# Channel attention on one core: how much of the packed blocks' room joins the ring of the second pass, and in what order rows leave

## The chip, the cores and the metric

One core of a Trainium2 chip runs the kernel; the other cores are idle. The metric is the device time of one execution in microseconds (us). A row below means one row of every partition: 128 pixels of 384 channels in bf16, 98,304 bytes. The input has 1152 such rows (113.25 MB), the output as many.

## The reference

```python
xf = x.reshape(B, H * W, C)          # x: (1, 384, 384, 384) bf16
gap = jnp.mean(xf, 1)
gmp = jnp.amax(xf, 1)
h_a = gap @ w1;  h_a = h_a * (h_a > 0)
h_m = gmp @ w1;  h_m = h_m * (h_m > 0)
scale = sigmoid(h_a @ w2 + h_m @ w2)
return x * scale[:, None, None, :]
```

The scale of each channel needs the mean and the maximum over all pixels, so every pixel must be seen before the first one can be multiplied. x doesn't fit on the chip's SBUF whole.

## The kernel before

**First pass.** All 1152 rows are read (SP issues, L356). For each piece PE adds the rows up (`sums`, L259), and DVE keeps a running maximum in `acc` (L325). What fits stays on the chip: the three slots of `body` (96 rows, `STAYING`), 21 rows in `held`, 11 in `acc`, 8 + 2 in PSUM, a few more, and seven *packed blocks*. A packed block is 32 rows kept in the room of 24: four parts a, b, w, d of 8 rows (G = 8) each. PE and ACT turn the high bytes of the four parts into codes of 4 bits, four codes to a 16-bit word, and the fourth part gives up its own room (`pack`, L301; its room in `held` is used again by the next block). 782 rows are let go and have to be read again (`PLACES`, `again`).

**Turn.** After the last row the mean, the maximum and the two small products give `scale_bc` (L387 to L417).

**Second pass.** `multiply` (L422, DVE) scales rows in place; stores are issued by ACT (`put`, L431; `store`, L474), reads by SP (`read`, L506). First the staying rows leave (`put`), in small pieces at the start (`FIRST_STORES`). As their room comes free, the 782 rows are read again into places of `body` that are handed out in the order of `PLACES`: this is the ring. Its turn number k takes the next place in order, multiplies, stores, issues the reads that have become possible, and then does the turn's job of `jobs`:

- `unpack(i, h)` (L446): half a packed block back to four parts: eight DVE operations (L452, L457), six copies on ACT (L471). Part d goes to a home in `held`, two homes in turn (`homes_d`).
- `finish(i)` (L478): multiplies the block's 24 rows and the 8 rows of part d, and stores both. After it the block's 24 rows of `body` may join the ring: `read` compares a place's end with `RING + 3 * G * blocks_gone`.

So the ring begins with 96 rows (RING) and grows by 24 with each finished block, and the later entries of `PLACES` are longer: 24, 30, 36, 48 rows, the last one 20. At turn 19 (`LEAVING_TURN`) the rows that were kept in PSUM are copied or multiplied into rows 222 and up of `body` (L549 to L553), and they are stored with the next turns. Everything on an engine stays in the written order (`manual_schedule`). Every DMA reports to one of eight semaphores in turn, and the issue of a DMA also waits until the one that had its semaphore before has landed. Last stands a branch (L555) that is taken only if the values didn't fit the packing; with this input it is not taken.

Of the kernel before, what the change touches and what calls it, by code (L numbers as in the profile page):

```python
# [32 lines left out]
RING = 96  # L33
G = 8
PACKED = 7
PSUM_ROWS = 8
LATE_ROWS = 8
BANK_ROWS = 2
# [14 lines left out]


PLACES = (
# [3 lines left out]
)  # L59
LEAVING_AT = 222  # L60
LEAVING_TURN = 19
FIRST_STORES = ((1, 2, 3, 4, 4, 5, 6, 6), (9, 10, 12), (16, 18))
HELD_STORES = (6, 7)
ACC_STORES_AT = 3
# [6 lines left out]
def kernel(  # L71
# [7 lines left out]
    nc = tc.nc  # L79
# [11 lines left out]
    xr = x.rearrange("b h w c -> (b h w) c")  # L91
    orr = out.rearrange("b h w c -> (b h w) c")

    def rows_of(ap, block):
        first, n = block
        return ap[first * P:(first + n) * P, :].rearrange("(p n) c -> p n c", n=n)
# [8 lines left out]
    def take(n):  # L105
        nonlocal at
        at += n
        return at - n, n

    ps_block = take(PSUM_ROWS)  # L110
    beside = take(BANK_ROWS + A)
    packed_block = take(GP * PACKED)
    held_block = take(sum(LAST_HELD))
# [7 lines left out]
    again = [take(n) for _, n in PLACES]  # L121


    small = consts.tile([P, 16], BF16)
# [18 lines left out]
    acc = consts.tile([P, A, C], BF16)  # L143
    nc.dynamic_dma_scratch_size = RING_BYTES
    nc.lookup_mloc("DynamicDMAScratchLoc").dims = [P, RING_BYTES]
    held = nc.alloc_sbuf_tensor_at("held", [P, HELD_ROWS, C], BF16, offset=RING_BYTES).ap()
    body = xpool.tile([P, RING + 3 * G * PACKED, C], BF16, name="body")
    slots = [body[:, SLOT * i:SLOT * i + stay[i][1], :] for i in range(NS)]
    spare = body[:, SLOT * NS, :]
    homes = [body[:, RING + 3 * G * i:RING + 3 * G * (i + 1), :] for i in range(PACKED)]  # L150
# [10 lines left out]
    kept_ps = psum.tile([P, PSUM_ROWS, C], BF16)  # L161
    words_ps = psum.tile([P, G, C], BF16)
    words = words_ps.rearrange("p n c -> p (n c)").bitcast(F32)
    late = words_ps[:, 0:LATE_ROWS, :]
# [7 lines left out]
    kept_b = bank_b[:, 0:C * BANK_ROWS // 2].bitcast(BF16).rearrange("p (n c) -> p n c", n=BANK_ROWS)  # L172
# [5 lines left out]
    in_order.enter_context(tc.manual_schedule(engines=None))  # L178

    nc.vector.memset(ones_bf, 1.0)  # L180
    nc.vector.memset(pick, 0.0)
    for q in range(CQ):
        nc.vector.memset(pick[q * QP:q * QP + 1, q:q + 1], 1.0)
# [32 lines left out]
    for i in range(PACKED):  # L216
        first, d_at = 3 * G * i, 3 * G * PACKED + G * i
# [20 lines left out]
    for block, buf, pieces in parts_left:  # L238
        for j, m in enumerate(pieces):
            lo = sum(pieces[:j])  # L240
# [86 lines left out]
    def turn_over(out_, rows):  # L327

        for r in range(LATE_ROWS):
            for q in range(CQ):  # L330
                nc.tensor.transpose(  # L331
                    out=out_[:, r, q * P:(q + 1) * P], in_=rows[:, r, q * P:(q + 1) * P], identity=ident_bf
                )
# [11 lines left out]
    for st in steps:  # L345
# [8 lines left out]
        _, block, rows, lo, hi = st  # L354
        m = hi - lo
# [8 lines left out]
        j = max(0, min(m, A - done))  # L364
# [41 lines left out]
    for q0, part_ps in tp_ps:  # L406
        n = part_ps.shape[1]
# [12 lines left out]
    def multiply(dst, src):  # L420
        n = dst.shape[1]
        nc.vector.tensor_tensor(  # L422
            out=dst, in0=src, in1=scale_bc.unsqueeze(1).to_broadcast([P, n, C]), op=ALU.mult
        )
# [13 lines left out]


    turns = len(PLACES)  # L440
    homes_d = [held[:, G * ((i + 1) % 2):G * ((i + 1) % 2 + 1), :] for i in range(PACKED)]
    HG = G // 2
    m = held[:, 2 * G:2 * G + HG, :]
    t = acc[:, G:G + HG // 2, :].rearrange("p n c -> p (n c)").bitcast(U8)
# [28 lines left out]
    def store(buf, block, lo):  # L473
        nc.scalar.dma_start(out=rows_of(orr, block)[:, lo:lo + buf.shape[1], :], in_=buf)  # L474

    d_at = 3 * G * PACKED

    def finish(i):  # L478

        for rows in (homes[i], homes_d[i]):  # L480
            multiply(rows, rows)
        store(homes[i], packed_block, 3 * G * i)
        store(homes_d[i], packed_block, d_at + G * i)


    jobs = [[(unpack, 0, 0)], [(unpack, 0, 1)]]
    for i in range(1, PACKED):
        jobs += [[(unpack, i, 0)], [(finish, i - 1)], [(unpack, i, 1)]]
    jobs.append([])
    jobs.append([(finish, PACKED - 1)])  # L490

    order = []
    turn_of_row = [-1] * (RING + 3 * G * PACKED)

    def read(last_turn, blocks_gone):

        if not again:
            return False
        k = len(PLACES) - len(again)
        lo, n = PLACES[k]  # L500
        if lo + n > RING + 3 * G * blocks_gone or max(turn_of_row[lo:lo + n]) > last_turn:
            return False
        turn_of_row[lo:lo + n] = [k] * n
        buf, b = body[:, lo:lo + n, :], again.pop(0)
        assert b[1] == n
        nc.sync.dma_start(out=buf, in_=rows_of(xr, b))  # L506
        order.append((b, buf))
        return True

    k = ACC_STORES_AT  # L510
    put(stay[0], slots[0], FIRST_STORES[0][:k])
    put_acc()
    j = sum(FIRST_STORES[0][:k])
    put(stay[0], slots[0][:, j:, :], FIRST_STORES[0][k:], j)
    put(held_block, held[:, LATE_ROWS:, :], HELD_STORES, LATE_ROWS)
    put(refill, held[:, 0:LATE_ROWS, :], (LATE_ROWS,))
    read(-1, 0)
    put(stay[1], slots[1], FIRST_STORES[1])
    read(-1, 0)
    put(stay[2], slots[2], FIRST_STORES[2])  # L520
    read(-1, 0)
    read(-1, 0)
    nc.vector.tensor_scalar(out=flag, in0=bad_ps, scalar1=0.5, scalar2=None, op0=ALU.is_gt)
    bad = nc.values_load(flag, engines=(ENG.SP, ENG.Activation, ENG.DVE))
    assert len(jobs) <= turns - 2
    leaving = []
    gone = 0
    for turn in range(turns):
        b, buf = order.pop(0)
        multiply(buf, buf)  # L530
        store(buf, b, 0)
        if leaving:
            to, block = leaving.pop(0)
            store(to, block, 0)
        while read(turn, gone):
            pass
        for job, *which in jobs.pop(0) if jobs else ():
            job(*which)
            gone += job is finish
        if turn == LEAVING_TURN:  # L540
            j = LEAVING_AT
            assert j >= max(lo + n for lo, n in PLACES) and gone > PACKED - 2
            for block, rows in ((ps_block, kept_ps[:, 0:PSUM_ROWS, :]), (held_block, late), (beside, kept_b)):
                n = rows.shape[1]
                leaving.append((body[:, j:j + n, :], block))
                j += n
            assert j <= RING + 3 * G * (PACKED - 1)
            to = leaving[1][0]
            nc.vector.tensor_copy(out=to.bitcast(U32), in_=late.bitcast(U32))  # L549
            turn_over(late, to)  # L550
            multiply(leaving[0][0], kept_ps[:, 0:PSUM_ROWS, :])
            multiply(leaving[2][0], kept_b)
            multiply(to, late)  # L553
    assert not again and not order and not jobs and not leaving
    with tc.If(bad != 0):  # L555
        for i in range(PACKED):
            for buf, lo in ((homes[i], 3 * G * i), (homes_d[i], d_at + G * i)):
                n = buf.shape[1]
# [33 lines left out]
```

## Time and profile before

| | |
|---|---|
| time, median of 3 (lowest to highest) | 731.45 us (731.15 to 733.26) |
| time of the profiled execution | 731.59 us |
| its span, first to last instruction | 729.8 us |
| busy in the span: DVE, ACT, PE | 563.1, 348.7, 186.4 us |
| moved by DMA | 305.63 MB, mean 419 GB/s over the span |
| of it read, written | 192.14 MB, 113.25 MB |
| second pass: first read issued, last read landed, last store issued | 290.1, 687.2, 696.2 us |

The profile gives busy times by engine, and the DMA's by sixteen DMA engines that share every transfer: a DMA share of 1.00 in a stretch means that all sixteen had a packet in hand all the time (it can come out a little above 1, because a packet is counted in the stretch in which it starts). GB/s beside it is what they moved. A wait names what ended it.

### The profile page before, as it was taken

The numbers are of one execution on the slowest core, as the hardware profiler recorded it, in microseconds if no ns is written. First come the engines' busy times: TensorE is split into PE (matmuls) and PEld (weight loads), VectorE is DVE, ScalarE is ACT, GpSimd is POOL, SyncE is SP. The second block draws the span as 40 slices with busy tenths as digits, with TensorE's granted clock in tenths as the row PEclk, the third lists the DMA queues.
The fourth block names the chain that finished last, engine by engine and source line by source line (L and its number), as shares of the span: only waits on it lengthen the run. The fifth ranks groups of instructions, "written<-read, shape, count | busy, mean of one in ns | idle before, by whom it ended". The sixth has DMA issues, their size and how long they took to land.

```text
span 729.8 us, 3860 instructions
## 1 busy us (share of the span) xinstructions
PE 186.4 (26%) x1357; PEld 73.0 (10%) x1357; DVE 563.1 (77%) x421; ACT 348.7 (48%) x251; POOL 0.7 (0%) x6
## 2 busy tenths in 40 slices
PE   5667576876768470000000000000000000010000
PEld 2222222322222140000000000000000000010000
DVE  6799999999999998959999595975865790059910
ACT  6979999999999100047245345080080063000000
POOL 0000000000000000000000000000000000000000
PEclk9878977998897555555555555555555555555555
DMA  9999999999999979999999999999999999999996
GB/s 381 434 425 419 438 420 439 423 434 425 426 430 423 418 298 356 395 434 425 433 427 438 434 424 429 431 438 425 435 435 428 431 431 443 419 436 425 430 423 293
DMA packets 21987, 305.63 MB, mean 419 GB/s; under 512 B 2800, under 2 KB 3408, under 8 KB 9552
## 3 DMA queue, kind: packets, MB, share of 16 engines
q1 hardware_dynamic: 13328, 192.14, 62.2%
q10 hardware_dynamic: 8640, 113.25, 36.4%
q8 instruction: 10, 0.16, 0.1%
q14 instruction: 9, 0.07, 0.0%
HBM read 192.14 MB, written 113.25 MB: 418 GB/s over the span
## 4 chain that ended last, share of the span: by engine, by line
DMA 59%; DVE 23%; another core or an unknown queue 6%; issue 3%; PE 2%; ACT 1%; SPq 0%; ACTq 0%; DVEq 0%
DMA body<-in_x_dram 42%; DMA out_dram<-body 17%; DVE body L422 11%; DVE acc L325 10%; PE words_ps L307 1%; PE bank_a L259 1%; DVE held L422 1%; ACT body L471 0%; ACT held L471 0%; SPq L356 0%; PE words_ps L331 0%; DVE acc L422 0%; DVE held L452 0%; DVE body L549 0%
## 5 line engine op out<-in xcount | busy, mean ns | idle before, releaser
L422 DVE TENSOR_TENSOR body<-body,scale_bc 128x9216 bf16<-128x9216 bf16 (+15 forms) x45 | 214.5, 4802 | 63.0 <-DMA body<-in_x_dram 60.2
L325 DVE TENSOR_TENSOR acc<-acc,body 128x2304 bf16<-128x2304 bf16 (+4 forms) x210 | 229.7, 1166 | 14.6 <-DMA body<-in_x_dram 14.5
L471 ACT COPY held<-body 128x1536 uint8<-128x1536 uint8 x14 | 20.6, 1475 | 202.8 <-DMA out_dram<-held 131.5
L259 PE MATMUL bank_a<-body,small 128*1 128x512 bf16 (+2 forms) x849 | 93.0, 481 | 83.8 <-DMA body<-in_x_dram 83.7
L331 PE MATMUL words_ps<-ident_bf,body 128*128 128x128 bf16 x24 | 2.7, 309 | 370.9 <-DVE body L549 370.9
L287 ACT ACTIVATE held<-held 128x3072 uint8<-128x3072 uint8 (+1 forms) x35 | 82.0, 2344 | 1.1
L286 ACT ACTIVATE held<-body,held 128x3072 uint8<-128x3072 int8 (+1 forms) x28 | 61.9, 2211 | 10.5 <-DMA body<-in_x_dram 10.0
L259 PEld LDWEIGHTS <-small 128*1 128x1 bf16 x891 | 30.4, 96 | 147.1 <-issue 131.6
L471 ACT COPY body<-acc 128x1536 uint8<-128x1536 uint8 x28 | 41.2, 1472 | 0.4
L331 PEld LDWEIGHTS <-body 128*128 128x128 bf16 x24 | 2.5, 144 | 371.2 <-issue 371.2
L307 PE MATMUL words_ps<-body,scale_bc 128*128 128x512 fp8e4 (+1 forms) x126 | 37.4, 409 | 3.7 <-ACT body L314 3.7
L549 DVE COPY body<-words_ps 128x1536 uint32<-128x1536 uint32 x1 | 1.8, 1757 | 43.5 <-DMA out_dram<-body 43.5
L307 PE MATMUL words_ps<-body,w_sb 128*128 128x512 fp8e3 x84 | 26.0, 392 | 0.0
L307 PE MATMUL words_ps<-held,body 128*128 128x512 fp8e4 x84 | 25.0, 379 | 0.0
L471 ACT COPY held<-acc 128x1536 uint8<-128x1536 uint8 x14 | 20.6, 1472 | 6.1 <-DVE acc L457 6.1
L471 ACT COPY body<-body 128x1536 uint8<-128x1536 uint8 x14 | 20.7, 1476 | 0.4
L313 ACT COPY body<-held 128x1536 uint8<-128x1536 uint8 x14 | 20.6, 1469 | 0.0
L471 ACT COPY acc<-body 128x1536 uint8<-128x1536 uint8 x14 | 20.5, 1466 | 0.0
L313 ACT COPY body<-body 128x1536 uint8<-128x1536 uint8 x14 | 20.4, 1460 | 0.0
L314 ACT ACTIVATE body<-words_ps 128x1536 uint16<-128x1536 f32 x14 | 20.1, 1438 | 0.0
L286 ACT ACTIVATE held<-held 128x3072 uint8<-128x3072 int8 x7 | 20.0, 2856 | 0.2
L325 DVE TENSOR_TENSOR acc<-acc,held 128x1920 bf16<-128x1920 bf16 (+4 forms) x18 | 17.5, 1008 | 0.1
(70 smaller groups left out, 190.3 us busy)
## 6 DMA issues: line engine op xcount, KB each, us to landing
body<-in_x_dram SPq DMA_DIRECT2D x20, 2976.0 KB, 21.7
out_dram<-body ACTq DMA_DIRECT2D x17, 2304.0 KB, 29.4
body<-in_x_dram SPq DMA_DIRECT2D x16, 2304.0 KB, 17.6
body<-in_x_dram SPq DMA_DIRECT2D x4, 4608.0 KB, 27.9
out_dram<-body ACTq DMA_DIRECT2D x4, 4608.0 KB, 32.0
body<-in_x_dram SPq DMA_DIRECT2D x6, 2880.0 KB, 20.1
body<-in_x_dram SPq DMA_DIRECT2D x5, 3456.0 KB, 20.0
out_dram<-body ACTq DMA_DIRECT2D x5, 3456.0 KB, 37.9
```

What stands on the lines that cost most here:

```text
L259: nc.tensor.matmul(sum_ps[q * QP:q * QP + 1, 0:g * P], lhsT=ones_bf[:, 0:1], rhs=rows[:, k:k + g, q * P:(q + 1) * P], start=(done + k == 0 ...
L286: nc.scalar.activation(out=out_, in_=rows, func=ACT.Square, bias=test_bias, scale=TEST_SCALE)
L287: nc.scalar.activation(out=out_, in_=out_, func=ACT.Square, bias=minus4, accum_out=tests[:, k:k + 1],)
L307: nc.tensor.matmul(words[:, c:c + BANK], lhsT=weights[2 * r + k], rhs=high(part(i, r), dt)[:, half * n + c:half * n + c + BANK], start=(r ...
L313: nc.scalar.copy(out=high(part(i, r), U8)[:, span], in_=low(part(i, r + 2), U8)[:, span])
L314: nc.scalar.activation(out=part(i, 2).rearrange("p n c -> p (n c)").bitcast(U16)[:, span], in_=words, func=ACT.Copy, bias=32767.5,)
L325: nc.vector.tensor_tensor(out=out_, in0=in0, in1=in1, op=ALU.max)
L331: nc.tensor.transpose(out=out_[:, r, q * P:(q + 1) * P], in_=rows[:, r, q * P:(q + 1) * P], identity=ident_bf)
L422: nc.vector.tensor_tensor(out=dst, in0=src, in1=scale_bc.unsqueeze(1).to_broadcast([P, n, C]), op=ALU.mult)
L471: nc.scalar.copy(out=dst, in_=src)
L549: nc.vector.tensor_copy(out=to.bitcast(U32), in_=late.bitcast(U32))
```

## The change

- The ring takes the room of block 0 alone, so it grows once, from 96 rows to 120 (`gone = gone or job is finish`). `PLACES` becomes nine places of 24 rows, then 18 of 30 and one of 26: 28 turns for the 25 of before, 782 rows as before.
- Blocks 2 to 6 are still unpacked and multiplied on the way, but their rows stay where they are and are stored in the last three turns: blocks 2 and 3 in one store of 48 rows, 4 and 5 in another, then 6.
- Part d gets five places. Blocks 0 to 2 use the two homes in `held`; d of blocks 3, 4 and 5 goes to block 1's room, which is free once block 1 has left; d of block 6 to `held`. Only d of blocks 0 to 2 is stored on the way.
- `jobs` has empty turns where a home must first come free.
- The rows kept in PSUM go to `held` and `acc`, three turns from the end, and are stored as the very last.
- The first read of the second pass, 24 rows, is issued in three pieces of 8 rows.
- Sixteen memsets of one unused element are put at the start of DVE's instructions (`FILLS`).

```diff
+PLACES = (
+    ((0, 24), (24, 24), (48, 24), (72, 24)) * 2 + ((96, 24),)
+    + ((0, 30), (30, 30), (60, 30), (90, 30)) * 4 + ((0, 30), (30, 30), (60, 26))
+)
-LEAVING_AT = 222
-LEAVING_TURN = 19
+FIRST_READ = (8, 8, 8)
+FILLS = 16
...
     nc.vector.memset(ones_bf, 1.0)
+    for _ in range(FILLS):
+        nc.vector.memset(small[0:1, 15:16], 0.0)
...
-    homes_d = [held[:, G * ((i + 1) % 2):G * ((i + 1) % 2 + 1), :] for i in range(PACKED)]
+    homes_d = [held[:, G * (i % 2):G * (i % 2 + 1), :] for i in (1, 0, 1)]
+    homes_d += [homes[1][:, G * i:G * (i + 1), :] for i in range(3)] + [held[:, 0:G, :]]
...
-        store(homes[i], packed_block, 3 * G * i)
-        store(homes_d[i], packed_block, d_at + G * i)
+        if i < 2:
+            store(homes[i], packed_block, 3 * G * i)
+        if i < 3:
+            store(homes_d[i], packed_block, d_at + G * i)
...
+    jobs = [[(unpack, 0, 0)], [(unpack, 0, 1)], [(unpack, 1, 0)], [(finish, 0)], [(unpack, 1, 1)], [], [(finish, 1)]]
+    jobs += [[(unpack, 2, 0)], [(unpack, 2, 1)], []]
+    for i in range(3, PACKED):
         jobs += [[(unpack, i, 0)], [(finish, i - 1)], [(unpack, i, 1)]]
...
+    after = [
+        [(body[:, RING + 3 * G * 2:RING + 3 * G * 4, :], 3 * G * 2)],
+        [(body[:, RING + 3 * G * 4:RING + 3 * G * 6, :], 3 * G * 4)],
+        [(homes[1], d_at + 3 * G), (homes_d[6], d_at + 6 * G), (homes[6], 3 * G * 6)],
+    ]
...
-        nc.sync.dma_start(out=buf, in_=rows_of(xr, b))
+        j = 0
+        for m in FIRST_READ if k == 0 else (n,):
+            nc.sync.dma_start(out=buf[:, j:j + m, :], in_=rows_of(xr, b)[:, j:j + m, :])
+            j += m
...
+    leaving = [(held[:, G:G + PSUM_ROWS, :], ps_block), (acc[:, 0:LATE_ROWS, :], held_block)]
+    leaving.append((acc[:, LATE_ROWS:LATE_ROWS + BANK_ROWS, :], beside))
     for turn in range(turns):
         b, buf = order.pop(0)
         multiply(buf, buf)
+        if turn >= turns - len(after):
+            for rows, lo in after[turn - turns + len(after)]:
+                store(rows, packed_block, lo)
         store(buf, b, 0)
-        if leaving:
-            to, block = leaving.pop(0)
-            store(to, block, 0)
         while read(turn, gone):
             pass
         for job, *which in jobs.pop(0) if jobs else ():
             job(*which)
-            gone += job is finish
-        if turn == LEAVING_TURN:
+            gone = gone or job is finish
+        if turn == turns - 3:
...
+    for to, block in leaving:
+        store(to, block, 0)
```

More of the change, by code (lines that the diff above doesn't have):

```diff
@@ L440 @@
     turns = len(PLACES)
-    homes_d = [held[:, G * ((i + 1) % 2):G * ((i + 1) % 2 + 1), :] for i in range(PACKED)]
+    homes_d = [held[:, G * (i % 2):G * (i % 2 + 1), :] for i in (1, 0, 1)]
+    homes_d += [homes[1][:, G * i:G * (i + 1), :] for i in range(3)] + [held[:, 0:G, :]]
+    assert len(homes_d) == PACKED
     HG = G // 2
@@ L481, in finish @@
             multiply(rows, rows)
-        store(homes[i], packed_block, 3 * G * i)
-        store(homes_d[i], packed_block, d_at + G * i)
-    jobs = [[(unpack, 0, 0)], [(unpack, 0, 1)]]
-    for i in range(1, PACKED):
+        if i < 2:
[5 more added lines that the diff above has]
+    for i in range(3, PACKED):
         jobs += [[(unpack, i, 0)], [(finish, i - 1)], [(unpack, i, 1)]]
@@ L505, in read @@
         assert b[1] == n
-        nc.sync.dma_start(out=buf, in_=rows_of(xr, b))
+        j = 0
+        for m in FIRST_READ if k == 0 else (n,):
+            nc.sync.dma_start(out=buf[:, j:j + m, :], in_=rows_of(xr, b)[:, j:j + m, :])
+            j += m
+        assert j == n
         order.append((b, buf))
@@ L524 @@
     bad = nc.values_load(flag, engines=(ENG.SP, ENG.Activation, ENG.DVE))
-    assert len(jobs) <= turns - 2
-    leaving = []
+    assert len(jobs) <= turns - 3
     gone = 0
+    leaving = [(held[:, G:G + PSUM_ROWS, :], ps_block), (acc[:, 0:LATE_ROWS, :], held_block)]
+    leaving.append((acc[:, LATE_ROWS:LATE_ROWS + BANK_ROWS, :], beside))
     for turn in range(turns):
@@ L538 @@
             job(*which)
-            gone += job is finish
-        if turn == LEAVING_TURN:
[L541 to L547, printed above, removed]
+            gone = gone or job is finish
+        if turn == turns - 3:
             to = leaving[1][0]
@@ L553 @@
             multiply(to, late)
-    assert not again and not order and not jobs and not leaving
+    assert not again and not order and not jobs
+    for to, block in leaving:
+        store(to, block, 0)
     with tc.If(bad != 0):
```

3 rows, old and new, of the table PLACES are left out of this document.

## The prediction

> **What bounds the kernel now.** I read the page first: DMA rows, then the chain, then the stretches of the second pass one by one.
>
> ```profile
> span 729.8 us, 3860 instructions
> ...
> DMA  9999999999999979999999999999999999999996
> ...
> q1 hardware_dynamic: 13328, 192.14, 62.2%
> q10 hardware_dynamic: 8640, 113.25, 36.4%
> ```
>
> Reads (q1) and stores (q10) together fill 98.6% of the sixteen DMA engines' span; DVE is at 77%. The chain of waits names DMA for 59% and DVE for 23%, but a chain only tells who released whom. The stretches tell whether DMA was ever short of work (columns: length; busy time of PE, PEld, DVE, ACT, POOL; clock, DMA share, GB/s):
>
> ```profile
> 266.00:282.00 16.00, 8.50 (x111) 7.16 (x108) 13.75 (x19) 1.78 (x7) 0.00 (x0) 0.50 0.62 224
> 282.00:290.00 8.00, 0.00 (x0) 0.00 (x0) 8.00 (x8) 0.00 (x0) 0.00 (x0) 0.50 1.01 401
> 290.00:300.00 10.00, 0.00 (x0) 0.00 (x0) 10.00 (x6) 0.00 (x0) 0.00 (x0) 0.50 1.01 365
> 300.00:340.00 40.00, 0.00 (x0) 0.00 (x0) 29.41 (x22) 17.10 (x12) 0.00 (x0) 0.50 1.01 430
> 340.00:400.00 60.00, 0.00 (x0) 0.00 (x0) 58.20 (x42) 26.87 (x20) 0.00 (x0) 0.50 1.01 431
> 600.00:645.00 45.00, 0.00 (x0) 0.00 (x0) 2.85 (x4) 7.54 (x6) 0.00 (x0) 0.50 0.99 425
> 645.00:690.00 45.00, 2.72 (x24) 2.48 (x24) 42.73 (x10) 0.00 (x0) 0.00 (x0) 0.50 1.02 436
> 700.00:722.00 22.00, 0.00 (x0) 0.00 (x0) 0.00 (x0) 0.00 (x0) 0.00 (x0) 0.50 1.00 430
> 722.00:729.00 7.00, 0.00 (x0) 0.00 (x0) 0.00 (x0) 0.00 (x0) 0.00 (x0) 0.50 0.26 111
> ```
>
> From 282 to 722 the share is 1.00 throughout, at 430 GB/s whether DVE works 97% of the time (340 to 400) or 6% (600 to 645), with reads and stores mixed or with stores alone (700 to 722). The kernel is bound by bytes. At 430 GB/s, 305.63 MB take 710.8 us; the span is 19 us longer. I find them at the turn (266 to 282: 16 x (1 - 224/430) = 7.7), in the slow stretch where the first read begins (290 to 300: 10 x (1 - 365/430) = 1.5, with the share at 1.01, so packets were slow, none missing), in small stores (282 to 290: 0.5), at the end (722 to 729.8: 7.8 us for 0.78 MB, which is 1.8 us of work, so 6.0), at the start (0 to 3: about 2.2), and 240 us of first pass at 427 GB/s (1.7). The bytes don't change. So the change can win only in these places, or lose by letting DMA run dry.
>
> **The change part by part.** The profiled execution took 731.59 us (span 729.8 and 1.8 around it), 0.14 above the median.
>
> *Sixteen memsets.* The memset of one element takes 59 ns by its row, three of them 0.27 us as issued: 16 x 0.09 = 1.4 us on DVE at its start. DVE idles 2.13 us there before the first rows land at 4.07; its memset of the bank that PE's sums need moves from 1.8 to 3.2, before PE's first matmul at 4.18; ACT's first activation reads `pick` and moves from 2.03 to about 2.6, its weights from 3.8 to 4.4, and ACT then waits until 8.72. Cost 0; uncovered, 1.4. They also shift DVE's code by sixteen instructions. Code comes over the same DMA engines:
>
> ```profile
> q10 hardware_dynamic: 197, 0.33, 91.3%
> q14 instruction: 1, 0.01, 4.8%
> ```
>
> This is the DMA view of 280 to 281 us, when the first stores begin: one packet of code takes 4.8% of 16 engine-microseconds, 0.77 us, on one engine. Sixteen DVE instructions earlier is about 270 us, in the gap, where engines are free. If the packet is DVE's, one engine is 0 to 0.77 earlier from there on; whether that engine ends last isn't shown. I take -0.3. The Trainium skill (Runtime: NRT & Kernel Launch, section Instruction fetch mechanics) says that code comes in blocks of 16 KiB and that crossing a block is mostly hidden; by it this term is 0 and the sum 0.3 higher. The trace has such packets (q8: 10 packets, 0.16 MB) and ones of half that size (q14).
>
> *First read in three pieces.* The read at 290.11 waits for the 6-row store issued at 286.08 and landed at 289.93. Its first 8 rows wait only for the store issued at 282.88 (4 rows, 384 KB, median 3.4 us to landing): 286.3; the next 8 for one issued at 284.81 (5 rows, 3.7 us): 288.5. But from 282 to 290 the share is 1.01: an earlier read takes the place of stores and adds nothing. From below, small pieces might spare the slow stretch: -1.5. From above, each piece might pay its own latency: 8 rows read alone (`held`, issued 272.43) took 4.0 us, for 0.79 MB, 1.8 us at 430; 2.2 us more each, +4.3 for two. The nearest row is the stores of 4 to 6 rows from 282 to 290, back to back without a gap: 0.
> The Trainium skill (DMA: Bandwidth & Descriptors, section Bandwidth) speaks against the pieces: it asks for 1 MiB and more per DMA. They have 0.75 MiB. The share of 1.01 says that here such costs lie beside other packets.
>
> *A smaller ring.* The stage with 24-row places already runs on four places, here from 300 to 360:
>
> ```profile
> body<-in_x_dram SPq DMA_DIRECT2D x5, 2304.0 KB, 17.6
> out_dram<-body ACTq DMA_DIRECT2D x5, 2304.0 KB, 21.0
> ```
>
> Read 17.6, multiply 4.95, store 21.0: 43.6 us, four turns of 10.9; 48 rows at 430 GB/s take 11.0. So DMA sets the turn, and the times to landing are mostly queue. A turn of 30 rows moves 60 rows, 13.7 us; four places give a cycle of 54.9. What a place needs at worst outside its own 13.7 us of transfer: DVE's job before it (finish, 4.95 + 1.75 = 6.7; half an unpack is 4 x 0.56 + 2 x 0.55 + 2 x 0.96 = 5.3), its multiply (6.16 by the row of 11520 elements), six ACT copies of 1.47 that may stand ahead of its store (8.8), and latency of 2.2 for each transfer: 26 us, of 41 that are there. DVE's fullest turn is 12.9, below 13.7. Cost 0. All lengths of place so far ran at 430 to 432 GB/s, so no term for them.
>
> *d's homes, the five blocks, the late rows.* ACT waits 131.5 us in five waits for homes of d; with five homes they go, and so do four stores (10 for 14 of the packed blocks) and this wait:
>
> ```profile
> 646.49 1.76 DVE L549 COPY body<-words_ps 128x1536 uint32<-128x1536 uint32 x1 [43.54 <-DMA out_dram<-body]
> ```
>
> For 43.5 us DVE stands still, since rows 222 and up are still being stored; ring reads that land are not multiplied. Yet DMA moves 425, then 436 GB/s, 430 over both: worth 0 to 0.5 us (45 x (1 - 425/430)); I take -0.2. What is late next is again DMA. Held back are 152 rows of blocks 2 to 6 (48 + 48 + 24 + 8 + 24), 18 late rows and about three places (86), some 256 rows, 58 us of stores with no read left. 700 to 722 shows that stores alone run at 430. ACT issues eleven stores there; by the eight semaphores the last waits for the second one of 48 rows, with 128 rows (29 us) still queued behind that. No gap.
>
> *The end.* From 722 the engines finish one by one (the same columns):
>
> ```profile
> 723.00:724.00 1.00, 0.00 (x0) 0.00 (x0) 0.00 (x0) 0.00 (x0) 0.00 (x0) 0.50 0.33 138
> ...
> 725.00:726.00 1.00, 0.00 (x0) 0.00 (x0) 0.00 (x0) 0.00 (x0) 0.00 (x0) 0.50 0.25 108
> 726.00:727.00 1.00, 0.00 (x0) 0.00 (x0) 0.00 (x0) 0.00 (x0) 0.00 (x0) 0.50 0.07 31
> ```
>
> Five of sixteen are left, then four, then one, until about 728; evenly spread, they would end at 723.8. The last engine carries what slow packets and code it happened to get. The change sorts none of this except by its first two parts: 0, between -3 and +3.
>
> **Sum:** -0.3 - 0.2 = -0.5: 731.1 from the profiled execution, **731.0** from the median.
>
> **Rivals.**
> 1. *The last engine catches up.* Without the slow stretch (1.5) and the code packet (0.77), and so with less lag, the end comes 2.2 to 4 us sooner: 728.4. For it: these are the losses that the pieces and memsets touch. Against: slow packets have no cause in the profile. 0.22.
> 2. *The ring runs dry, slower.* Place: the turns of 30 rows with jobs, thirteen of them, when no finished block's stores fill the queue any more (before, 32 rows in every third turn). It decides once a place needs over 41 us outside its transfers, or DVE over 13.7 a turn; DVE's mean of 6.16 + 5.7 = 11.9 leaves 1.8. If waits between ACT and DVE take that and 0.3 more in each: +4, 735.5. For it: DVE idled 3.9 us before each 30-row multiply (19.6 in five). Against: those waits were for DMA, at a full share. 0.14.
> 3. *The pieces pay their latency* one after the other, at the first read: +4.3, 735.8. Against: the share of 1.01 there. 0.03. The Trainium skill's rule on DMA size (DMA: Bandwidth & Descriptors, section Bandwidth) points this way.
> 4. *The parts do nothing:* code packet and slow stretch stay. 731.5. 0.05.
>
> **How the numbers follow.** My forecast has the remaining 0.56, with 729.3 to 733.5 as its own range; 0.3% (2.2 us) is about what a measurement of this kernel can tell from no change. Of the 0.56 I give 0.50 to within, 0.03 to each side. Faster: 0.22 + 0.03 = 0.25; same: 0.50 + 0.05 = 0.55; slower: 0.14 + 0.03 + 0.03 = 0.20. The range goes from inside rival 1 to rival 2's value: 727.5 to 735.5; what lies outside, the far halves of 1 and 2 and rival 3, is under 0.2.
>
> **What would show it.** Right: DMA share 1.00 at 430 GB/s from 282 to the last 6 us; no wait of 43 us on DVE; no code packet of q14 between 278 and 290; first read issued near 286.3; last read landed near 670. Rival 1: the tail after the share falls under 0.9 is 4 us or less. Rival 2: slices under 0.95 between 400 and 640. Wrong altogether: another rate than 430 GB/s for stores alone over 50 us, or for one length of place over hundreds.

## The result and the profile after

The changed kernel takes 728.77 us (median of 6 runs, 728.14 to 729.43) beside 731.89 us (731.15 to 733.26) for the kernel before. The ratio is 0.9956, 95% interval 0.9943 to 0.9969: 3.1 us faster. The time lies in the forecast's range, but the likeliest case of the forecast, 731.0 and "within 0.3%", did not happen. Rival 1's time, 728.4, is the nearest.

The profiled execution of the changed kernel took 729.27 us. Its page, with the lines that answer to those of before:

```profile
span 727.5 us, 3877 instructions
...
DMA  9999999999999979999999999999999999999997
...
q1 hardware_dynamic: 14048, 192.14, 62.3%
q10 hardware_dynamic: 8496, 113.25, 36.5%
```

The bytes are the same, in 720 packets more for the reads and 144 fewer for the stores; the span is 2.3 us shorter. The stretches (length; busy time of PE, PEld, DVE, ACT, POOL; clock, DMA share, GB/s):

```profile
282.00:290.00 8.00, 0.00 (x0) 0.00 (x0) 8.00 (x8) 0.00 (x0) 0.00 (x0) 0.50 1.01 366
290.00:300.00 10.00, 0.00 (x0) 0.00 (x0) 10.00 (x5) 0.00 (x0) 0.00 (x0) 0.50 1.02 414
300.00:340.00 40.00, 0.00 (x0) 0.00 (x0) 33.15 (x28) 18.86 (x14) 0.00 (x0) 0.50 1.01 427
340.00:400.00 60.00, 0.00 (x0) 0.00 (x0) 52.69 (x29) 19.21 (x14) 0.00 (x0) 0.50 1.00 431
600.00:645.00 45.00, 0.00 (x0) 0.00 (x0) 27.25 (x9) 7.17 (x5) 0.00 (x0) 0.50 1.00 431
645.00:690.00 45.00, 2.74 (x24) 2.48 (x24) 23.23 (x7) 0.00 (x0) 0.00 (x0) 0.50 1.01 436
700.00:722.00 22.00, 0.00 (x0) 0.00 (x0) 0.00 (x0) 0.00 (x0) 0.00 (x0) 0.50 0.99 425
722.00:729.00 7.00, 0.00 (x0) 0.00 (x0) 0.00 (x0) 0.00 (x0) 0.00 (x0) 0.50 0.22 89
723.00:724.00 1.00, 0.00 (x0) 0.00 (x0) 0.00 (x0) 0.00 (x0) 0.00 (x0) 0.50 0.47 183
725.00:726.00 1.00, 0.00 (x0) 0.00 (x0) 0.00 (x0) 0.00 (x0) 0.00 (x0) 0.50 0.03 11
726.00:727.00 1.00, 0.00 (x0) 0.00 (x0) 0.00 (x0) 0.00 (x0) 0.00 (x0) 0.50 0.00 0
```

In the stretches shown between 300 and 722 little changed: the share is 0.99 to 1.01 at 425 to 436 GB/s, and before it was 0.99 to 1.02 at 425 to 436. The slow stretch did not go, it moved with the first read, from 290 to 300 (365 GB/s) into 282 to 290 (366). From 282 to 300, 8 x 366 + 10 x 414 = 7,068 KB were moved, against 8 x 401 + 10 x 365 = 6,858 before: 0.5 us of work at 430 GB/s. The rest of the gain stands in the last lines. Before, engines were at work until 728; now the share is 0.03 at 725 to 726 and nothing follows.

The landing records of the trace show this engine by engine, since each DMA reports once from each of the sixteen. In the kernel before, the first engine ends its part of the last store at 723.3, the sixteen on average at 724.5, the last at 728.4. Now it is 723.1, 723.9 and 725.8. I call the distance from mean to last the **lag**: 3.9 us before, 1.9 after. The experiments below are read by these two numbers, the mean end (how long the work took) and the lag (how unevenly it fell).

### The profile page after: what moved, and what is told of

Same layout as the page of the kernel before. It is cut to its first block, busy times and chain, and to the rows that moved or that the text cites. A ratio compares the mean times of both kernels' runs of the same rounds, so it can differ in the third digit from the quotient of the medians.

```text
span 727.5 us, 3877 instructions
## 1 busy us (share of the span) xinstructions
PE 189.8 (26%) x1357; PEld 73.9 (10%) x1357; DVE 565.0 (78%) x440; ACT 349.5 (48%) x251; POOL 0.7 (0%) x6
## 4 chain that ended last, share of the span: by engine, by line
DMA 64%; DVE 26%; issue 2%; PE 1%; SPq 0%; ACT 0%; DVEq 0%; ACTq 0%
DMA body<-in_x_dram 47%; DMA out_dram<-body 17%; DVE body L423 13%; DVE acc L326 10%; DVE held L423 1%; PE words_ps L308 1%; DVE held L455 1%; PE bank_a L260 0%; DVE acc L423 0%; DVE acc L460 0%; DVE body L460 0%; DVE kept_ps L380 0%; DVE body L455 0%; DVE acc L455 0%; DVE acc L367 0%
## 5 line engine op out<-in xcount | busy, mean ns | idle before, releaser
L423 DVE TENSOR_TENSOR body<-body,scale_bc 128x11520 bf16<-128x11520 bf16 (+14 forms) x51 | 220.2, 4352 | 90.3 <-DMA body<-in_x_dram 87.5
L332 PE MATMUL words_ps<-ident_bf,acc 128*128 128x128 bf16 x24 | 2.7, 313 | 375.9 <-DVE acc L560 375.9
L474 ACT COPY body<-body 128x1536 uint8<-128x1536 uint8 x20 | 29.5, 1477 | 93.5 <-DVE body L423 93.1
L474 ACT COPY held<-body 128x1536 uint8<-128x1536 uint8 x8 | 11.8, 1476 | 100.8 <-DVE body L423 59.8
L474 ACT COPY body<-acc 128x1536 uint8<-128x1536 uint8 x34 | 49.6, 1475 | 8.0 <-DVE acc L460 7.6
L332 PEld LDWEIGHTS <-acc 128*128 128x128 bf16 x24 | 2.5, 147 | 376.3 <-DVE acc L560 376.3
L308 PE MATMUL words_ps<-body,scale_bc 128*128 128x512 fp8e4 (+1 forms) x126 | 39.4, 427 | 2.7 <-ACT body L315 2.7
L314 ACT COPY body<-body 128x1536 uint8<-128x1536 uint8 x14 | 20.5, 1463 | 0.0
L308 PE MATMUL words_ps<-body 128*128 128x512 fp8e3 x42 | 16.5, 394 | 0.0
L455 DVE TENSOR_SCALAR held<-held 128x1536 uint16<-128x1536 uint16 x28 | 15.7, 560 | 1.0
```

The lines of the kernel that those rows point to most:

```text
L308: nc.tensor.matmul(words[:, c:c + BANK], lhsT=weights[2 * r + k], rhs=high(part(i, r), dt)[:, half * n + c:half * n + c + BANK], start=(r ...
L314: nc.scalar.copy(out=high(part(i, r), U8)[:, span], in_=low(part(i, r + 2), U8)[:, span])
L332: nc.tensor.transpose(out=out_[:, r, q * P:(q + 1) * P], in_=rows[:, r, q * P:(q + 1) * P], identity=ident_bf)
L423: nc.vector.tensor_tensor(out=dst, in0=src, in1=scale_bc.unsqueeze(1).to_broadcast([P, n, C]), op=ALU.mult)
L455: nc.vector.tensor_scalar(out=u16(dst), in0=u16(src), scalar1=s1, scalar2=s2, op0=op0, op1=op1)
L474: nc.scalar.copy(out=dst, in_=src)
```

## The experiments

Names with a_ are edits of the changed kernel, names with b_ of the kernel before. "Rows" is the longest read of the second pass. Mean end and lag come from one profiled execution each, the ratio from runs beside the kernel before on the same chip (its medians there: 731.3 to 731.9). Executions of one kernel lie between 0.7 us (a_ring96, five of them) and 5.1 us (before, 31) apart, which is as much as the lags differ. So one lag or one mean end is one draw, and only what holds over several kernels is read from them.

| kernel | rows | time, us | ratio [95%] | mean end | lag |
|---|---|---|---|---|---|
| before | 48 | 731.89 | 1 | 724.5 | 3.9 |
| b_both | 48 | 731.26 | 0.9992 [0.9982, 1.0002] | 723.9 | 3.7 |
| b_late_rows | 48 | 732.37 | 1.0008 [0.9996, 1.002] | 724.8 | 5.0 |
| b_split | 30 | 731.84 | 1.0008 [0.9997, 1.0019] | 726.6 | 1.5 |
| b_even30 | 30 | 733.91 | 1.0037 [1.0025, 1.0049] | 729.6 | 0.7 |
| b_even30_late | 30 | 730.95 | 0.999 [0.9979, 1.0] | 725.5 | 1.6 |
| b_ring120 | 30 | 730.49 | 0.9992 [0.9982, 1.0003] | 724.7 | 2.3 |
| a_neither | 30 | 729.99 | 0.9974 [0.9961, 0.9988] | 724.1 | 2.8 |
| a_one_read | 30 | 729.42 | 0.9973 [0.9964, 0.9982] | 724.3 | 2.2 |
| a_no_fills | 30 | 729.66 | 0.9972 [0.9962, 0.9982] | 724.5 | 1.5 |
| a_leave_at_once | 30 | 729.1 | 0.9968 [0.9955, 0.9981] | 724.4 | 1.5 |
| a_all24 | 24 | 729.74 | 0.9978 [0.9967, 0.9989] | 724.1 | 2.1 |
| a_ring96 | 24 | 728.44 | 0.996 [0.9947, 0.9973] | 724.0 | 0.7 |
| after | 30 | 728.77 | 0.9956 [0.9943, 0.9969] | 723.9 | 1.9 |

### First four: is it the turn or the ring?

My theory after the result was that the two small parts at the turn (memsets, pieces) bring the gain; the rival was the ring, with all that goes with it.

*a_neither*: both small parts out.

```diff
-FIRST_READ = (8, 8, 8)
-FILLS = 16
+FIRST_READ = (24,)
+FILLS = 0
```

> The changed kernel without the sixteen memsets and with the first read whole: the ring, the five blocks and d's homes alone. Theory T (the turn): the gain comes from the turn alone, where one DMA engine fell 2.6 us behind by 309 us (0.6 from the code packet, 2.0 during the first read) and in the changed kernel only 0.5; the ring is worth nothing. Then this kernel is as slow as before: 731 to 732, ratio 0.999 to 1.001. Theory R (the ring): the smaller ring and the late blocks bring the gain, since no wait of 43 us is left on DVE and lengths are equal. Then it stays near the changed kernel: about 728.8, ratio 0.996.

0.9974: the ring alone, with the late blocks, the new homes of d and the late rows, brings 1.9 us. The theory of the turn fails as the whole cause. Its stretches at the turn are those of the kernel before:

```profile
282.00:290.00 8.00, 0.00 (x0) 0.00 (x0) 8.00 (x8) 0.00 (x0) 0.00 (x0) 0.50 1.01 402
290.00:300.00 10.00, 0.00 (x0) 0.00 (x0) 10.00 (x6) 0.00 (x0) 0.00 (x0) 0.50 1.01 368
```

*b_both*: the two small parts alone, put into the kernel before.

```diff
     nc.vector.memset(ones_bf, 1.0)
+    for _ in range(16):
+        nc.vector.memset(small[0:1, 15:16], 0.0)
...
-        nc.sync.dma_start(out=buf, in_=rows_of(xr, b))
+        j = 0
+        for m in (8, 8, 8) if k == 0 else (n,):
+            nc.sync.dma_start(out=buf[:, j:j + m, :], in_=rows_of(xr, b)[:, j:j + m, :])
+            j += m
```

> The kernel before, with its own ring, and with the sixteen memsets and the first read in three pieces. Theory T: all of the gain, 728.5 to 729.3, ratio 0.996. Theory R: no gain, 731.5 to 732, ratio 1.000.

0.9992, an interval that holds 1: on the old ring the small parts are most likely worth 0.6 us, and no more than 1.3. Here the turn looks like that of the changed kernel, so they did what they do there:

```profile
282.00:290.00 8.00, 0.00 (x0) 0.00 (x0) 8.00 (x8) 0.00 (x0) 0.00 (x0) 0.50 1.01 357
290.00:300.00 10.00, 0.00 (x0) 0.00 (x0) 10.00 (x6) 0.00 (x0) 0.00 (x0) 0.50 1.02 416
```

*a_no_fills* (`FILLS = 0`) and *a_one_read* (`FIRST_READ = (24,)`): one of the two out.

> The changed kernel without the sixteen memsets. If the code packet of DVE counts, it is back near 280.6 us and one engine starts the second pass 0.6 us late: about 0.6 slower than the changed kernel, 729.4, ratio 0.997. If the packet starts more than itself (the late engine also falls behind in the first read), up to 2.6 slower: 731.4. If it is nothing (mostly hidden): 728.8.

> The changed kernel with the first read whole, the memsets kept. If the slow stretch of the first read comes from its size, one engine falls 2 us behind there again: 730.5 to 731, ratio 0.998 to 0.999. If the pieces are worth nothing, as I forecast, 728.8, ratio 0.996.

0.9972 and 0.9973: with one of the two out, the time is that of a_neither. Both together take the ratio from 0.9974 to 0.9956, 1.3 us, with intervals that overlap. So these runs give neither part a value of its own.

### Next four: which part of the ring?

Three theories: the lengths of the places (L), DVE's wait of 43.5 us (W), the blocks kept for the end (B).

*a_leave_at_once*: blocks 2 to 6 and every part d are stored at their finish.

```diff
-        if i < 2:
-            store(homes[i], packed_block, 3 * G * i)
-        if i < 3:
-            store(homes_d[i], packed_block, d_at + G * i)
+        store(homes[i], packed_block, 3 * G * i)
+        store(homes_d[i], packed_block, d_at + G * i)
...
-        if turn >= turns - len(after):
-            for rows, lo in after[turn - turns + len(after)]:
-                store(rows, packed_block, lo)
```

> The changed kernel, but every unpacked block and its part d leave at their finish, so that the reads' last 55 us hold mixed traffic as before and no five blocks are left for the end. Three theories of the ring's share of the gain (1.9 us of 3.1): L, that equal and shorter places (24 and 30 rows in place of 24 to 48) keep the 16 transfer engines together, gives 728.8 (ratio to the kernel before 0.996): nothing is lost. W, that DVE's wait of 43.5 us for a buffer let the last engine fall behind, also gives 728.8, as that wait stays away. B, that the blocks left for the end give a tail of stores alone in which a late engine catches up, gives 730.7 (0.9984): the ring's gain is gone and the small parts' stays.

729.1, 0.9968. The interval holds the changed kernel's 0.9956 and ends at 0.9981, short of the 0.9984 that B asked for: the late blocks are worth 0.9 us by the ratios, anything from 0 to 1.8 by the interval. Nor does a tail of stores alone even the engines out. Here it is shorter (the last read lands at 694.6, in the changed kernel at 675.3), and the lag is 1.5. In the changed kernel the last engine is 2.7 us behind the first in the first store that lands after the last read, and still 2.7 in the last one: over 45 us of stores alone it doesn't catch up.

*b_late_rows*: the kernel before with the PSUM rows leaving last.

```diff
+    leaving = [(held[:, 0:PSUM_ROWS, :], ps_block), (acc[:, 0:LATE_ROWS, :], held_block)]
+    leaving.append((acc[:, LATE_ROWS:LATE_ROWS + BANK_ROWS, :], beside))
...
-        if turn == LEAVING_TURN:
...
+        if turn == turns - 3:
...
+    for to, block in leaving:
+        store(to, block, 0)
```

> The kernel before, but the 18 PSUM rows are worked on three turns ahead of the end, in held and acc, and leave last, as in the changed kernel: DVE's wait of 43.5 us for the room of these rows is gone, the ring and the blocks are as before. W: 730.0, ratio 0.9974. L and B: 731.9, ratio 1.000.

1.0008: W falls. The longest wait of DVE in the second pass went and nothing came of it.

*b_even30*: the kernel before with 30-row places from the tenth read on.

```diff
-    (0, 30), (30, 30), (60, 30), (90, 30), (120, 24), (0, 36), (36, 36), (72, 36), (108, 36), (144, 48),
-    (0, 48), (48, 48), (96, 48), (144, 36), (192, 30), (0, 20),
+    (0, 30), (30, 30), (60, 30), (90, 30), (120, 30), (0, 30), (30, 30), (60, 30), (90, 30), (120, 30), (150, 30), (0, 30), (30, 30), (60, 30), (90, 30), (120, 30), (150, 30), (180, 30), (0, 26),
```

> The kernel before with its growing ring, but every place from the tenth read on has 30 rows (none of 36 or 48; the last has 26), three more reads in all. The PSUM rows still leave as before, with their stores right behind turn 19. L (lengths): 730.0, ratio 0.9974. W (DVE's wait for the reads of the late rows' places): 731.9 if the wait stays, and between the two if the shorter places shorten it; the trace says which. B (late blocks): 731.9, ratio 1.000.

733.91, slower; no theory had that. The stretches show why:

```profile
630.00:640.00 10.00, 2.72 (x24) 2.48 (x24) 9.23 (x5) 0.00 (x0) 0.00 (x0) 0.50 0.94 397
640.00:645.00 5.00, 0.00 (x0) 0.00 (x0) 5.00 (x2) 0.00 (x0) 0.00 (x0) 0.50 0.50 147
645.00:650.00 5.00, 0.00 (x0) 0.00 (x0) 5.00 (x2) 0.00 (x0) 0.00 (x0) 0.50 1.05 373
```

Here the queue did run dry: 10 x 0.06 + 5 x 0.50 = 3.1 us lost. It follows DVE's wait for the room of the PSUM rows, which the waits of the same kernel (us in total, times, longest) put at 36.8:

```profile
DVE body L548 <- DMA out_dram<-body: 36.8, 1, 36.8
```

The hole also lined the engines up: the last one's distance from the first fell from 2.8 us in the store that landed at 642 to 0.4 in the one at 661. At the end it is 0.9, and all engines are still at work at 726 to 727:

```profile
726.00:727.00 1.00, 0.00 (x0) 0.00 (x0) 0.00 (x0) 0.00 (x0) 0.00 (x0) 0.50 1.11 479
```

So an even end is not worth anything if all engines paid for it.

*a_all24*: the changed kernel with 24-row places throughout, five of them.

```diff
-    + ((0, 30), (30, 30), (60, 30), (90, 30)) * 4 + ((0, 30), (30, 30), (60, 26))
+    + ((0, 24), (24, 24), (48, 24), (72, 24), (96, 24)) * 4 + ((0, 24), (24, 24), (48, 24), (72, 14))
```

> The changed kernel with places of 24 rows throughout (five places in place of four, last read of 14 rows). L (shorter pieces keep the engines together): 728.3 to 728.8, ratio 0.995 to 0.996, with the last engine at most 1.9 us behind the mean. W and B say nothing for shorter pieces: 728.8. Against all of them, if the ring's depth in rows (120 in place of 120, but five reads under way in place of four) matters: no more than 0.3 either way.

729.74, 0.9978: no better, by the ratios rather 1.6 us worse than the changed kernel (the intervals just meet). Shorter than 30 rows brings no more by itself.

### Last four: lengths or depth?

S says that the gain comes from a shallow ring.

*b_even30_late*: the edits of b_even30 and b_late_rows together, so that the hole is closed.

> The kernel before with two edits of the last batch together: 30-row places from the tenth read on (the ring still grows, to 236 rows), and the 18 PSUM rows leaving last. Each alone did not gain (b_even30 lost about 3 us to a hole in the traffic near 640 us, and then its engines ended within 0.9 us of each other; b_late_rows changed nothing). L, equal and shorter places are the gain and the hole was the price of the PSUM rows' wait: 730.0, ratio 0.9974, last engine's lag at the end at most 3.5 us. S, the gain comes from the shallow ring (at most 120 rows under way or waiting), not from the lengths: 731.9 to 732.4, ratio 1.000, lag 5 or more.

0.999: without the hole, 30-row places bring the lag from 3.9 to 1.6, as L has it, but the time most likely by only 0.7 us: the mean end is 1.0 later, with the share at 0.99 and more in every stretch of 20 us from 300 to 722.

*b_ring120*: the kernel before with the changed kernel's `PLACES`, and `LEAVING_TURN = 22`.

> The kernel before with only the places of the changed kernel (120 rows, reads of 24 and 30), the PSUM rows put three turns later because there are three turns more; the blocks leave at their finish, the parts d and the PSUM rows have their old places, no small parts. S and L both: 730.0, ratio 0.9974. Neither: 731.9, and then the ring's gain needs the parts' new places or the late rows beside it.

0.9992: the interval leaves out the 0.9974 that S and L both asked for. So the places alone, shallow and short, do not bring what a_neither gains, though the lag fell to 2.3. (The two intervals still overlap, from 0.9982 to 0.9988.)

*b_split*: the places of before; a turn's reads and stores above 30 rows go as two DMAs each. Those of 30 rows stay whole, so the largest packets are of 23,040 bytes and not of 24 rows, as was expected.

```diff
-        nc.sync.dma_start(out=buf, in_=rows_of(xr, b))
+        h = n // 2 if n > 30 else n
+        for j in range(0, n, h):
+            nc.sync.dma_start(out=buf[:, j:j + h, :], in_=rows_of(xr, b)[:, j:j + h, :])
...
-        store(buf, b, 0)
+        h = buf.shape[1] // 2 if buf.shape[1] > 30 else buf.shape[1]
+        for j in range(0, buf.shape[1], h):
+            store(buf[:, j:j + h, :], b, j)
```

> The kernel before with its places, but every read and every store of 36 and 48 rows goes as two DMAs of half the length, so that no packet of the second pass is above 24 rows. If the length of one packet (36,864 bytes at 48 rows, near 1.5 us) is what sets the engines apart, 730.0 and the lag between 600 and 640 us no longer grows by 5; if what counts is how far the ring lets reads run ahead (S), or the number of turns, 731.9.

1.0008, no gain, and yet the lag fell to 1.5: in the store that lands at 637 the last engine is 4.4 us behind the first, where the kernel before has 8.5 in the one at 631. What the lag gave, the mean took, which is 2 us later. Part of it stands in these stretches, at a full share:

```profile
500.00:520.00 20.00, 0.00 (x0) 0.00 (x0) 9.99 (x6) 6.96 (x5) 0.00 (x0) 0.50 1.00 415
520.00:540.00 20.00, 0.00 (x0) 0.00 (x0) 19.90 (x8) 10.13 (x8) 0.00 (x0) 0.50 1.00 420
```

The kernel before has 428 and 440 GB/s there. The records of the single packets tell more. Call the median time of a packet of one size, over all fourteen traces, its usual time, and count what packets took beyond it. From 500 to 540 that is 1.0 us per engine here and 0.1 in the kernel before; from 300 to the end it is 2.4 and 1.2. So slow packets cost about 1.2 us of the 2. The usual times of this kernel's more and shorter packets sum up to 1.2 us more as well (18,432 bytes take 686 ns, 36,864 take 1,364, a little less than twice that). Why packets are slow, no run tells.

*a_ring96*: the changed kernel with four places of 24 rows and no block's room at all.

```diff
-    ((0, 24), (24, 24), (48, 24), (72, 24)) * 2 + ((96, 24),)
-    + ((0, 30), (30, 30), (60, 30), (90, 30)) * 4 + ((0, 30), (30, 30), (60, 26))
+    ((0, 24), (24, 24), (48, 24), (72, 24)) * 8 + ((0, 14),)
```

> The changed kernel with a ring of 96 rows: four places of 24 throughout, no block's room joins. S taken further: shallower is no worse, 728.8 or less, as long as reads and stores stay queued. The prediction's rival of a ring that runs dry: slices under 0.95 between 400 and 640 us and 731 or more. L: the same as a_all24, 729.7.

728.44, 0.996: as fast as the changed kernel (its interval covers the other's value), with less room and a simpler list. It does not run dry, and ends most evenly of all:

```profile
400.00:640.00 240.00, 0.00 (x0) 0.00 (x0) 181.97 (x103) 80.14 (x56) 0.00 (x0) 0.50 1.01 431
...
723.00:724.00 1.00, 0.00 (x0) 0.00 (x0) 0.00 (x0) 0.00 (x0) 0.00 (x0) 0.50 0.54 209
724.00:725.00 1.00, 0.00 (x0) 0.00 (x0) 0.00 (x0) 0.00 (x0) 0.00 (x0) 0.50 0.06 20
725.00:726.00 1.00, 0.00 (x0) 0.00 (x0) 0.00 (x0) 0.00 (x0) 0.00 (x0) 0.50 0.00 0
```

### What the fourteen kernels say together

The lag sorts by the longest read: 3.7 to 5.0 us with reads of 36 and 48 rows (three kernels), 0.7 to 2.8 without them (eleven), whatever else differs (stores of 48 rows remain in most a_ kernels, as their last ones). That is the part of L that stands, as two things that go together in one execution each. It isn't shown as a cause: the three kernels share one list of places, a turn's store is as long as its read and was never varied alone, and no run shows what long transfers do to the engines. Slow packets don't cost more there: 1.2 to 1.5 us per engine from 300 on in the three kernels, 0.7 to 3.0 in the others.

When the lag arises can be told. In all fourteen kernels the last engine's distance from the first is the same, within 0.1 us, in every store that lands wholly after the last read has landed, to the end (5.1 us in the kernel before, 2.7 after), and no packet of that time takes 20 ns more than usual. So the lag is settled when the last read has landed, and all slow packets come before.

The lag is not the whole of the time. The a_ kernels have their mean end at 723.9 to 724.5. Of the others b_both is there (723.9) and the kernel before at its edge (724.5); b_even30, with its hole, is at 729.6, the remaining four at 724.7 to 726.6. So the kernels of the old stage with shorter reads gave back in the mean part of what they won in the lag, or all of it. Three things remain open: whether and how long reads set the engines apart, why b_split and b_even30_late have more slow packets (0.8 us per engine of b_even30_late's 1.0 are theirs), and how the 1.9 us of a_neither split among the places, the late blocks and d's homes (the homes were not tried alone). The single steps are of the size of one interval, about 0.1%.

## Why the prediction was right in part

**Bound by bytes: right.** Share and rate from 300 to 722 are those of before, and the mean end moved by 0.6 us.

**Sixteen memsets, -0.3: right in what they do.** The packet of code that sat at 280 to 281 is now in the gap, at 275 to 276, later than the 270 that I had estimated. The DMA view of that microsecond:

```profile
q1 hardware_dynamic: 89, 0.36, 94.0%
q14 instruction: 1, 0.01, 2.0%
```

In a_no_fills it is still found at 280 to 281, so the memsets move it:

```profile
q14 instruction: 1, 0.01, 3.5%
```

That is 0.56 us on one engine. The Trainium skill (Runtime: NRT & Kernel Launch, section Instruction fetch mechanics) has such a fetch mostly hidden. The trace shows it beside a busy queue, where its engine pays; the runs can't tell its price from 0.

**First read in pieces, 0: right for that stretch.** The three pieces were issued at 285.8, 288.3 and 292.4 (I had 286.3 and 288.5 for two) and landed at 292.2, 296.0 and 301.2, where the one read of before landed at 303.3. No latency was paid in series: rival 3 is out. The Trainium skill's rule of 1 MiB and more per DMA (DMA: Bandwidth & Descriptors, section Bandwidth) does not decide here. Pieces of 0.75 MiB cost nothing that the runs show, with the share at 1.01.

What I missed is that the two small parts also leave the engines closer together: once the first stores have landed, near 312, the last engine is 0.3 to 0.9 us behind the first in the seven kernels with one part or both, and 0.8 to 2.6 in the seven without (by the landing records). Those seven issue the same DMAs up to there, so 0.8 to 2.6 is also how far executions of one schedule differ.

**A smaller ring, 0: the step that failed.** It did not run dry, as worked out; rival 2 did not happen, and even 96 rows suffice. What failed is the sentence "All lengths of place so far ran at 430 to 432 GB/s, so no term for them". GB/s over a stretch is the mean of sixteen engines. As a mean the sentence holds (1,364 ns for 36,864 bytes is 27.0 bytes per ns, 686 ns for 18,432 is 26.9), but it says nothing of the spread, which only the end shows, and with the long reads of before the spread was larger. Together with "The change sorts none of this except by its first two parts: 0, between -3 and +3", this put the 1.9 us of a_neither outside the sum and left it in the bounds. So what failed is the 0 for the ring, with the -0.2 for what goes with it: together they measured -1.9 us. Which part brings them stays open, since b_ring120, with the places alone, does not show them.

**DVE's 43.5 us, -0.2: right that it was worth next to nothing.** Its wait is gone and b_late_rows gains nothing. In the changed kernel DVE waits longer in all, on reads, and nothing depends on that:

```profile
DVE body L423 <- DMA body<-in_x_dram: 87.5, 21, 13.5
```

**Late blocks, no gap: right.** 700 to 722 ran at 425 GB/s and a share of 0.99. The last read landed at 675.3, not 670.

**Rival 1** gave the time and the sign (a tail of 4 us or less; it is 2.8, from 723 to 725.8) for about two fifths of the reason: of the 3.2 us that the ratio 0.9956 means, 1.9 came with the ring and 1.3 with the two small parts on top of it. Its other conditions did not hold: the slow stretch moved and did not go, and the last engine does not catch up once the reads are over. So it is in good part luck that its time came out nearest, and the measured time lies in the range because of the room that the range left for rival 1, not because of the sum. Even so it deserved more than 0.22, since the prediction's own list had 6.0 us at the end, more than at any other place that the change touched.

## What to carry to other kernels

When all DMA engines are busy throughout, look at how far apart they finish: mean and last landing of the final transfer are two numbers, and the second can be lowered without moving a byte less. Here it was settled by the time the last read had landed. Long reads (36 and 48 rows, 3.5 and 4.7 MB each) went with 3.7 to 5.0 us of lag, reads of 30 rows and less with 0.7 to 2.8. Before crediting a smaller lag, check the mean end: a hole evened out the end too (b_even30) and cost 2.7 us by its ratio, and in b_split slow and shorter packets took back all that the lag gave.

## What the hardware showed that I had not expected

- With all sixteen engines at a full share from 300 to 720, the first and the last ended between 1.4 us (a_ring96) and 6.5 us (b_late_rows) apart.
- The dip in rate follows the first read wherever it begins: 365 GB/s at 290 to 300 with one read at 290, 366 at 282 to 290 with the first piece at 285.8, at shares of 1.01.
- One hole of 3.1 us (b_even30) brought all engines back within 0.4 us of each other.
- Once the last read had landed, the distance between first and last engine stood still within 0.1 us in every one of the fourteen kernels, over 23 to 53 us of stores alone.
